# Windowed attention feeding a gated feed-forward layer: weight loads, two casts, one copy and one batch's preparation moved in the order of work

## The chip, the cores and the metric

The kernel runs on one core of a Trainium2 chip. The metric is device time in microseconds (us); lower is better. Before the change, eight runs gave a median of 257.36 us (256.04 to 259.91). The profile shown below is of one execution that took 257.31 us.

## The reference

For 4 batches of 8 heads, 768 positions and head size 64, in fp32, attention is computed in which a query sees the first 4 positions and the 128 positions that end with itself; then a gated feed-forward layer runs over the 3072 tokens:

```
keep   = is_sink | in_window            # first 4 keys, or 0 <= q - k < 128
scores = where(keep, q @ k.T / 8, -1e9)
a      = softmax(scores);  x = (a @ v) with the heads side by side     # [3072, 512]
out    = (relu(x @ w_gate) * (x @ w_val)) @ w_out                      # d_ff = 1536
```

## The kernel before

**Units and stages.** Two heads make a *pair*; a batch has four pairs, so there are 16 units U0 to U15, four for each batch. Scores are formed only where the mask keeps them: keys are taken in seven overlapping tiles of 128. A unit passes these stages:

- its keys and queries are loaded in fp32 (`load_rows`, L159, through SyncE's DMA queue, called SP) and cast to bf16 by GpSimd (POOL) into `kn`, `qn` (`cast_rows`, L164);
- they are transposed. For batches 0 and 1 TensorE does it (`T_half`, `T`, L248), and ScalarE or VectorE copies the result from PSUM to SBUF (L258 the keys, L259 the queries). For batches 2 and 3 the casts are written to DRAM (`to_dram`, L169, "td") and come back by a transposing DMA (`turn`, L174), both on SP;
- `odd_tiles` (L183) has GpSimd copy some key columns once more, with the 4 sink keys in front;
- `Sg` (L279) forms scores for a third of the unit, ScalarE takes the exponential (L298) and VectorE multiplies by the mask (L300); these are S00, S01, S02 for the first pair of a batch, S10 to S12 for the second, and so on;
- `W` (L310) multiplies by the values `vn`; VectorE normalises (L330, L331). The values come in seven tiles j, each loaded by SP into one buffer `vf` (`load_v`, "lv") and cast by GpSimd (L134, "v");
- `X` (L334) transposes the result on TensorE and ScalarE copies it to `xT` (L345); for batches 2 and 3 it goes through DRAM instead (`x_to_dram` "xd", `x_turn` "xturn").

**The feed-forward part** is cut into 96 `chunk`s (L351), called slots: 24 for each batch, each with 4 products with the gate weights and 4 with the value weights (L362), a ReLU on ScalarE (L373) and a multiplication on VectorE (L375). Batch 0 is slots 0 to 23, batch 1 24 to 47, batch 2 48 to 71. Its second matrix product (`ffn2`, L400) is spread over later slots, three products a slot. The attention of batch b+1 is interleaved with the chunks of batch b: `plan` says after which slot which step stands, `prep` says before which slot a load, cast or copy is issued.

**What sets the order.** The order is written out by hand, and each engine, and each DMA queue, takes its own instructions in this order. A wait therefore holds everything behind it on that engine or queue. Three places matter here:

- GpSimd issues the weight loads itself (L190, L194), between its casts and copies.
- `pair()` (L239) hands out two PSUM tiles by turns. `T` takes one for its queries, and each `Sg` takes the next: after T of the third pair (T2) come S02 and then S10, and S10 gets the tile that T2's queries were in.
- In slots 0 and 8 the last pair's `X` stands in the middle of the chunk (`mid`): two gate and two value products come before it, the others after it. The fourth product of each kind reads what that `X` writes.

For units 8 and 9 the loads wait for a one-element write by VectorE (`gate`, L136), which stands in VectorE's order at the slot of the load.

In `prep`, a unit's four times are rows (load), castrows, td and turn. `rows` of unit 12, the first of batch 3, is at slot 30 throughout. Within a slot, units stand in rising order.

Of the kernel before, what the change touches and what calls it, by code (L numbers as in the profile page):

```python
# [21 lines left out]
def kernel(  # L22
# [12 lines left out]
    nc = tc.nc  # L35
# [5 lines left out]
    KO = d_model // 128  # L41
# [16 lines left out]
    qT = [x[:, 0:S] for x in KQ]  # L58
# [6 lines left out]
    wg = const.tile([128, KO, d_ff], BF16, name="wg")  # L65
    wv = const.tile([128, KO, d_ff], BF16, name="wv")
    wo = const.tile([128, FM, d_model], BF16, name="wo")
# [40 lines left out]
    half = lambda bufs, c: bufs[c // 2 % len(bufs)][:, c % 2 * HALF:c % 2 * HALF + HALF]  # L108
# [74 lines left out]
    def odd_tiles(u, copy):  # L183
        e = kE[u.i % NT]
        copy(odd(e)[:, :, 4:128], e[:, 120:876].rearrange("d (i c) -> d i c", c=252)[:, :, 0:124])  # L185
        sinks(u, copy)
# [52 lines left out]
    def pair():  # L239
        rot[0] += 1  # L240
        return PP[rot[0] % 2]
# [6 lines left out]
    def T(u):  # L248
        t = u.i % NT
        tk, tq = G[3][:], pair()[:, 0, :]  # L250
        for x, ps in ((kn[u.i % 2], tk), (qn[u.i % 2], tq)):
            for n in range(NR):
                c = slice(128 * n, 128 * n + 128)
                nc.tensor.transpose(ps.bitcast(BF16)[:, c], x[:, c], ident[:])
        vk, vq = (ps.bitcast(BF16)[:, 0:S].rearrange("d (n p) -> d p n", p=128) for ps in (tk, tq))
        e = kE[t]
        to = lambda ap: ap.rearrange("d (p n) -> d p n", n=NR)
        nc.scalar.copy(to(e[:, 0:S]), vk)  # L258
        (nc.scalar.copy if u.p < 2 else nc.vector.tensor_copy)(to(qT[t]), vq)  # L259
        odd_tiles(u, nc.gpsimd.tensor_copy)  # L260

    def T_half(c, banks=None, keys=nc.scalar.copy, queries=nc.vector.tensor_copy):
# [71 lines left out]
    def X(u, part=None, bank=None, copy=nc.scalar.copy):  # L334

        if bank is None:
            bank = G[3][:] if u.b == 0 or u.p < 2 else pair()[:, 0, :]
        ps = bank.bitcast(BF16)
        tiles, q0, q1 = PART[part]
        c = 0  # L340
        for t in tiles:
            nc.tensor.transpose(ps[:, c:c + 128], xn[u.i % 2][:, t, :], ident[:])  # L342
            c += 128 - t % 2 * 4
        c = 0 if part == 1 else 8
        copy(xT[u.b % 2][:, u.p, q0:q1], ps[:, c:c + q1 - q0])  # L345
        for x in range(2) if part is None else (part,):
            ready[u.b, u.p, x] = True
# [3 lines left out]
    def chunk(b, g, m, mid=None):  # L351

        x, h = xT[b % 2], hT[b % 2]
        cut = CUT if b else CUT0
        c = slice(0, cut) if g == 0 else slice(cut, S)
        n = c.stop - c.start
        gp, vp = G[gvn[0] % 3], G[(gvn[0] + 1) % 3]
        gvn[0] += 2

        def products(w, ps, kos):  # L360
            for ko in kos:
                nc.tensor.matmul(out=ps[:, 0:n], lhsT=w[:, ko, m * 128:(m + 1) * 128], rhs=x[:, ko, c],  # L362
                                 start=ko == 0, stop=ko == KO - 1)

        k0 = 2 if mid else 0
        if mid:
            products(wg, gp, range(k0))
            products(wv, vp, range(k0))
            mid()
        assert all((b, p, g) in ready for p in range(NP)), (b, g)  # L370
        products(wg, gp, range(k0, KO))
        gs = gspool.tile([128, S - CUT0], F32, name="gs")
        nc.scalar.activation(gs[:, 0:n], gp[:, 0:n], Act.Relu, bias=0.0, scale=1.0)  # L373
        products(wv, vp, range(k0, KO))
        nc.vector.tensor_tensor(h[:, m, c], gs[:, 0:n], vp[:, 0:n], op=Alu.mult)  # L375
# [31 lines left out]
    with tc.manual_schedule():  # L407
# [81 lines left out]
                for y in w.split():  # L489
                    put(s, y, b)  # L490
        prep = [[] for _ in slots]
        prep[1] += [("half", 6), ("half", 7), ("w", 6, 8), ("setup3",), ("v", 0, 3), ("v", 0, 4), ("v", 0, 5), ("v", 0, 6)]
        prep[4] += [("load", 4), ("load", 5), ("load", 6)]
        prep[8] += [("kq", 4), ("load", 7), ("lv", 1)]
        prep[9] += [("kq", 5), ("w", 8, 12)]
        prep[10] += [("kq", 6)]
        prep[11] += [("kq", 7)]
        prep[14] += [("v", 1, 0), ("v", 1, 1), ("v", 1, 2), ("v", 1, 3), ("wo",), ("v", 1, 4), ("v", 1, 5), ("v", 1, 6)]
        for i, ts in ((8, (18, 21, 22, 25)), (9, (19, 22, 23, 27)), (10, (21, 24, 25, 29)), (11, (23, 25, 27, 31)),
                      (12, (30, 33, 35, 38)), (13, (32, 35, 37, 40)), (14, (34, 37, 39, 43)), (15, (36, 39, 41, 45))):  # L500
            for t, what in zip(ts, ("rows", "castrows", "td", "turn")):
                prep[t].append((what, i))
            assert at["S", i - NP, 2] < ts[3] < at["S", i, 0] - 1, i
            prep[at["S", i, 0] - 1].append(("sinks", i))
            prep[at["W", i, 0] + 1].append(("xd", i))
            prep[at["W", i, 0] + 3].append(("xturn", i))

        for b, s0, s1 in ((2, 24, 28), (3, 44, 47)):
            for j in range(7):
                prep[s0 + j].append(("lv", b, j))  # L510
                prep[s1 + j].append(("v", b, j))

        f2 = deque()
        mid = {0: lambda: X(U[3], 0, g0), 8: lambda: X(U[3], 1)}
        for s, (b, g, m) in enumerate(slots):
            for x in prep[s]:
# [32 lines left out]
                else:  # L549
                    cast_v(*x[1:])  # L550
            chunk(b, g, m, mid.pop(s, None))
            if s == 23:
                f2 += [lambda t=t, mm=mm: ffn2(0, t, mm) for t in range(6) for mm in range(FM)]
            for what, i, x in plan[s]:
                if what == "F":
                    for _ in range(i):
                        f2.popleft()()
                elif what == "X":
                    X(U[i], x if i < NP else None)
                elif what == "T":  # L560
                    T(U[i])
                elif what == "H":
                    T_half(NP + i, queries=nc.scalar.copy if i == 0 else nc.vector.tensor_copy)
                elif what == "S":
                    Sg(U[i], x)
                else:
                    W(U[i], x if i < NP else None)
# [43 lines left out]
```

## Time and profile before

| what | value |
|---|---|
| the profiled execution's own time | 257.31 us |
| its span, first to last instruction | 255.3 us |
| TensorE (PE) busy | 241.3 us, 95% |
| weight loads on TensorE (PEld) | 140.8 us, 55% |
| VectorE (DVE) / ScalarE (ACT) / GpSimd (POOL) busy | 116.9 / 120.4 / 70.1 us |
| DMA | 40.07 MB, mean 157 GB/s |
| granted TensorE clock, mean | 0.984 |

By stretches of the span, in us:

| stretch | what runs | PE busy | ACT busy | POOL busy | DMA share |
|---|---|---|---|---|---|
| 0 to 20 | batch 0, first scores | 14.53 | 10.24 | 13.67 | 1.03 |
| 20 to 42.5 | slots 0 to 8 | 21.48 | 15.45 | 11.19 | 1.15 |
| 42.5 to 66 | slots 9 to 19, batch 1's T and S | 21.96 | 20.23 | 17.21 | 0.77 |
| 66 to 77 | slots 20 to 23, batch 1's W and X | 11.00 | 4.16 | 3.31 | 1.09 |
| 77 to 102 | slots 24 to 35, batch 2's S | 25.00 | 13.34 | 8.11 | 1.09 |
| 102 to 136 | batch 2's W, batch 3's loads | 31.81 | 13.39 | 9.79 | 0.99 |
| 136 to 160 | batch 3's S | 23.58 | 13.94 | 6.82 | 0.50 |

PE's busy time is modelled at the ends of matmuls, and stretches of matmuls overlap in it. A DMA share near or above 1 says that the 16 DMA engines had packets under way all the time. In rows of a timeline the first number is the start in us from the span's start, the second how long the row lasted; brackets hold the idle time of the engine before it and what ended that.

### The profile page before, as it was taken

Reading aid. Unit: us, or ns where it says so; the run is one execution under the profiler, and the core shown is the slowest. Engines: PE = TensorE matmul, PEld = TensorE weight load, DVE = VectorE, ACT = ScalarE, POOL = GpSimd, SP = SyncE. Lnnn points to the kernel's source line nnn. Section 1 sums busy time; section 2 is a strip of 40 time slices with the busy share of each in tenths; the row PEclk is TensorE's granted clock in tenths of the full one; section 3 lists DMA queues with packets and bytes.
Section 4 is the critical chain, followed back from the end, with each engine's and each line's share of the span. In section 5 each row is a group of like instructions: output and inputs, shape, how many; then the busy total and the mean of one; then the engine's idle time right before and its main releaser. Section 6 shows DMA issues by size and latency. Waiting matters only on the chain.

```text
span 255.3 us, 5322 instructions
## 1 busy us (share of the span) xinstructions
PE 241.3 (95%) x2084; PEld 140.8 (55%) x2084; DVE 116.9 (46%) x225; ACT 120.4 (47%) x219; POOL 70.1 (27%) x125
## 2 busy tenths in 40 slices
PE   7869999899999999699999999999999999999994
PEld 2444676555775555466655556666555555555443
DVE  5561794488872354467424455654223222322000
ACT  3744976789453385255234673622333233333111
POOL 7744941949054322733001720000000000000000
PEclk9995999999999999999999999999999999999999
DMA  6999999964999999999999902334210011110232
GB/s 214 223 202 259 200 371 236 183 111 67 194 384 283 251 216 253 256 315 255 165 237 218 203 3 64 88 89 121 74 44 17 24 41 44 44 41 0 85 122 83
DMA packets 75681, 40.07 MB, mean 157 GB/s; under 512 B 53512, under 2 KB 72712, under 8 KB 75656
## 3 DMA queue, kind: packets, MB, share of 16 engines
q1 hardware_dynamic: 67560, 34.10, 51.4%
q0 software_dynamic: 6864, 4.72, 12.7%
q10 hardware_dynamic: 1232, 0.92, 1.1%
q8 instruction: 16, 0.26, 0.4%
q14 instruction: 9, 0.07, 0.1%
HBM read 28.48 MB, written 11.25 MB: 156 GB/s over the span
## 4 chain that ended last, share of the span: by engine, by line
PE 71%; DMA 11%; SPq 7%; issue 5%; POOL 2%; ACT 1%; DVE 1%; ACTq 0%; POOLq 0%; DVEq 0%
PE g L362 39%; PE g L400 19%; DMA qf<-in_q_dram 7%; SPq L131 5%; PE pp L325 4%; PE pp L290 3%; PE pp L400 3%; DMA kf<-in_k_dram 3%; DMA vf<-in_v_dram 1%; SPq L113 1%; POOL qn L166 1%; SPq L175 1%; ACT ee L298 1%; SPq L161 1%; PE pp L394 1%
## 5 line engine op out<-in xcount | busy, mean ns | idle before, releaser
L375 DVE TENSOR_TENSOR hT<-gs,g 128x384 bf16<-128x384 f32 (+2 forms) x96 | 53.0, 552 | 92.4 <-PE g L362 87.4
L373 ACT ACTIVATE gs<-g 128x384 f32<-128x384 f32 (+2 forms) x96 | 47.5, 495 | 74.7 <-PE g L362 73.5
L362 PE MATMUL g<-xT,wg 128*128 128x384 bf16 (+2 forms) x384 | 79.9, 329 | 1.5 <-DMA wg<-in_moe_w_gate_dram 0.9
L362 PE MATMUL g<-xT,wv 128*128 128x384 bf16 (+2 forms) x384 | 79.7, 330 | 1.4 <-DMA wv<-in_moe_w_val_dram 1.3
L400 PE MATMUL g<-wo,hT 128*128 128x512 bf16 x240 | 64.0, 379 | 0.2 <-ACT ot L404 0.2
L362 PEld LDWEIGHTS <-wg 128*128 128x128 bf16 x384 | 36.3, 99 | 31.4 <-DMA wg<-in_moe_w_gate_dram 1.0
L362 PEld LDWEIGHTS <-wv 128*128 128x128 bf16 x384 | 37.7, 99 | 28.3 <-issue 2.3
L298 ACT ACTIVATE ee<-pp 128x838 bf16<-128x838 f32 (+4 forms) x50 | 43.1, 904 | 12.6 <-PE pp L290 12.4
L300 DVE TENSOR_TENSOR ee<-ee,msk 128x838 bf16<-128x838 bf16 (+3 forms) x44 | 32.4, 743 | 13.5 <-ACT ee L298 13.2
L400 PEld LDWEIGHTS <-hT 128*128 128x128 bf16 x276 | 25.5, 98 | 23.6 <-issue 0.4
L134 POOL CAST vn<-vf 128x512 bf16<-128x512 f32 x27 | 18.5, 704 | 24.5 <-DMA vf<-in_v_dram 24.3
L325 PEld LDWEIGHTS <-ee 128*128 128x128 bf16 x512 | 17.9, 97 | 4.9 <-issue 2.9
L404 ACT COPY ot<-g 128x512 f32<-128x512 f32 x20 | 11.7, 587 | 17.5 <-PE g L400 17.5
L325 PE MATMUL pp<-vn,ee 128*128 128x65 bf16 x488 | 17.8, 193 | 2.2 <-POOL vn L134 2.2
L290 PEld LDWEIGHTS <-KQ 64*128 64x128 bf16 x328 | 11.0, 94 | 11.5 <-issue 8.8
L166 POOL CAST kn<-kf 128x768 bf16<-128x768 f32 x12 | 10.4, 869 | 25.0 <-DMA kqd<-kn 9.4
L331 DVE TENSOR_TENSOR xn<-pp,rn 128x896 bf16<-128x896 f32 (+2 forms) x18 | 17.0, 943 | 0.6
L290 PE MATMUL pp<-KQ 64*128 64x3 bf16 (+5 forms) x316 | 16.2, 222 | 0.8 <-DVE KQ L259 0.6
L166 POOL CAST qn<-qf 128x768 bf16<-128x768 f32 x12 | 11.1, 924 | 2.3 <-DMA qf<-in_q_dram 1.9
L185 POOL COPY KQ<-KQ 128x372 bf16<-128x372 bf16 x12 | 6.4, 534 | 16.7 <-ACT KQ L258 9.8
L345 ACT COPY xT<-g 128x372 bf16<-128x372 bf16 (+2 forms) x10 | 5.4, 544 | 8.9 <-PE g L342 8.9
L400 PE MATMUL pp<-wo,hT 128*128 128x512 bf16 x36 | 8.1, 379 | 0.0
(80 smaller groups left out, 106.8 us busy)
## 6 DMA issues: line engine op xcount, KB each, us to landing
out_dram<-ot SPq DMA_DIRECT2D x23, 256.0 KB
kf<-in_k_dram SPq DMA_DIRECT2D x12, 384.0 KB
qf<-in_q_dram SPq DMA_DIRECT2D x12, 384.0 KB
vf<-in_v_dram SPq DMA_DIRECT2D x12, 256.0 KB
vf<-in_v_dram SPq DMA_DIRECT2D x12, 224.0 KB
kf<-in_k_dram SPq DMA_DIRECT2D x8, 192.0 KB
wo<-in_moe_w_out_dram POOLq DMA_DIRECT2D x3, 512.0 KB, 7.6
kqd<-qn SPq DMA_DIRECT2D x8, 192.0 KB
```

The lines of the kernel that those rows point to most:

```text
L131: nc.sync.dma_start(out=vf[a0:a1, j, :, :], in_=v[b, :, s0:s0 + a1 - a0, :].rearrange("h s d -> s h d"))
L134: copy(vn[b % 2][0:rows, j, :, 0:64], vf[0:rows, j, :, :])
L166: nc.gpsimd.tensor_copy(dst[u.i % 2][:].rearrange("p (n h d) -> p h n d", n=NR, h=2), src[u.i % NQ][:].rearrange("p (h n d) -> p h n d", n ...
L290: nc.tensor.matmul(out=at[h][:, c0:c1], lhsT=kE[t][64 * h:64 * h + 64, x0:x0 + 128], rhs=qT[t][64 * h:64 * h + 64, q0:q0 + c1 - c0], start ...
L298: nc.scalar.activation(x, ps[:, :, b0:n], Act.Exp, bias=0.0, scale=scale)
L300: nc.vector.tensor_tensor(x, x, msk[:, g, b0:n].unsqueeze(1).to_broadcast([128, 2, n - b0]), op=Alu.mult)
L325: nc.tensor.matmul(out=at[h][:, c:c + 65], lhsT=ee[u.i % NE][:, g, h, c0:c0 + 128], rhs=vn[u.b % 2][:, j, 2 * u.p + h, 0:65], start=c == 0 ...
L331: nc.vector.tensor_tensor(x.rearrange("p t (h d) -> p h t d", h=2), o[:, :, :, 0:64], r.unsqueeze(3).to_broadcast([128, 2, n, 64]), op=Alu ...
L362: nc.tensor.matmul(out=ps[:, 0:n], lhsT=w[:, ko, m * 128:(m + 1) * 128], rhs=x[:, ko, c], start=ko == 0, stop=ko == KO - 1)
L373: nc.scalar.activation(gs[:, 0:n], gp[:, 0:n], Act.Relu, bias=0.0, scale=1.0)
L375: nc.vector.tensor_tensor(h[:, m, c], gs[:, 0:n], vp[:, 0:n], op=Alu.mult)
L400: nc.tensor.matmul(out=op, lhsT=hT[b % 2][:, m, t * 128:(t + 1) * 128], rhs=wo[:, m, :], start=m == 0, stop=m == FM - 1)
```

## The change

Six places are edited.

1. `chunk` with a `mid`: after the `X`, the third gate and the third value product now both come before the fourth gate product (slots 0 and 8).
2. Slot 1: the load of weight blocks 6 and 7 stands in GpSimd's order between the cast of half 6 and that of half 7, in place of after both.
3. Slot 8: the cast of unit 5 ("batch 1's second cast") and the load of weight blocks 8 to 11 move from slot 9 to slot 8. On GpSimd they now stand ahead of the odd-tile copies of unit 4.
4. The queries of batch 1's third pair (unit 6) are copied from PSUM by ScalarE in place of VectorE (L259).
5. The load of the output weights moves from slot 14, where it stood among the value casts, to slot 13; on GpSimd it stands ahead of the odd-tile copies of unit 7.
6. Batch 2: rows, castrows, td and turn of units 8 to 11 are each a slot sooner, and so are the loads of batch 2's values (their casts stay). Unit 12's rows stay at slot 30: SP now has unit 11's turn ahead of them, and the first output tile and the last values' load also change places with their neighbours there.

```diff
-        (nc.scalar.copy if u.p < 2 else nc.vector.tensor_copy)(to(qT[t]), vq)
+        (nc.scalar.copy if u.p < 3 else nc.vector.tensor_copy)(to(qT[t]), vq)
...
         assert all((b, p, g) in ready for p in range(NP)), (b, g)
+        if mid:
+            products(wg, gp, range(k0, KO - 1))
+            products(wv, vp, range(k0, KO - 1))
+            k0 = KO - 1
         products(wg, gp, range(k0, KO))
...
-        prep[1] += [("half", 6), ("half", 7), ("w", 6, 8), ("setup3",), ("v", 0, 3), ("v", 0, 4), ("v", 0, 5), ("v", 0, 6)]
+        prep[1] += [("half", 6), ("w", 6, 8), ("half", 7), ("setup3",), ("v", 0, 3), ("v", 0, 4), ("v", 0, 5), ("v", 0, 6)]
         prep[4] += [("load", 4), ("load", 5), ("load", 6)]
-        prep[8] += [("kq", 4), ("load", 7), ("lv", 1)]
-        prep[9] += [("kq", 5), ("w", 8, 12)]
+        prep[8] += [("kq", 4), ("load", 7), ("lv", 1), ("kq", 5), ("w", 8, 12)]
         prep[10] += [("kq", 6)]
         prep[11] += [("kq", 7)]
-        prep[14] += [("v", 1, 0), ("v", 1, 1), ("v", 1, 2), ("v", 1, 3), ("wo",), ("v", 1, 4), ("v", 1, 5), ("v", 1, 6)]
-        for i, ts in ((8, (18, 21, 22, 25)), (9, (19, 22, 23, 27)), (10, (21, 24, 25, 29)), (11, (23, 25, 27, 31)),
+        prep[13] += [("wo",)]
+        prep[14] += [("v", 1, 0), ("v", 1, 1), ("v", 1, 2), ("v", 1, 3), ("v", 1, 4), ("v", 1, 5), ("v", 1, 6)]
+        for i, ts in ((8, (17, 20, 21, 24)), (9, (18, 21, 22, 26)), (10, (20, 23, 24, 28)), (11, (22, 24, 26, 30)),
                       (12, (30, 33, 35, 38)), (13, (32, 35, 37, 40)), (14, (34, 37, 39, 43)), (15, (36, 39, 41, 45))):
...
-        for b, s0, s1 in ((2, 24, 28), (3, 44, 47)):
+        for b, s0, s1 in ((2, 23, 28), (3, 44, 47)):
```

## The prediction, made before the change was run

> **What bounds the kernel now.** I read the page, the waits of PE, PE's timeline at each wait, and then the timelines of the engine or queue that ended it.
>
> ```profile
> PE 241.3 (95%) x2084; PEld 140.8 (55%) x2084; DVE 116.9 (46%) x225; ACT 120.4 (47%) x219; POOL 70.1 (27%) x125
> ...
> PEclk9995999999999999999999999999999999999999
> DMA  6999999964999999999999902334210011110232
> ```
>
> PE is the bound: 255.3 - 241.3 = 14.0 us idle is all that moving work can win. Slices are 6.38 us; DMA has room only in slices 8 and 9 (51 to 64 us) and after 140. PE's waits by releaser:
>
> ```profile
> PE pp L325 <- POOL vn L134: 2.2, 2, 1.3
> ...
> PE g L254 <- POOL kn L166: 0.7, 1, 0.7
> PE g L362 <- ACT xT L345: 0.7, 2, 0.4
> PE pp L290 <- DVE KQ L259: 0.6, 1, 0.6
> ...
> PE pp L254 <- POOL qn L166: 0.3, 1, 0.3
> ```
>
> These add up to 4.5 us, and each is touched. The other idle time lies before 20 us, in gaps too short to be listed, and at the end. The biggest wait, batch 2's first W (102.2 to 105.1 us), is ended by GpSimd:
>
> ```profile
> 101.58 0.83 POOL L166 CAST kn<-kf 128x768 bf16<-128x768 f32 x1 [4.96 <-DMA kf<-in_k_dram]
> 102.56 0.83 POOL L166 CAST qn<-qf 128x768 bf16<-128x768 f32 x1
> 103.33 0.61 POOL L134 CAST vn<-vf 128x512 bf16<-128x512 f32 x1
> ...
> 104.46 0.61 POOL L134 CAST vn<-vf 128x512 bf16<-128x512 f32 x1
> ```
>
> The last two value tiles stand behind unit 12's cast, which GpSimd awaits for 4.96 us: the load, not the cast, is late. SP shows why:
>
> ```profile
> 92.13 3.02 SPq L175 DMA_TRANSPOSE KQ<-kqd  x1
> 95.20 1.22 SPq L131 DMA_DIRECT2D vf<-in_v_dram  x3
> 96.46 0.56 SPq L161 DMA_DIRECT2D kf<-in_k_dram  x1
> 97.06 0.46 SPq L161 DMA_DIRECT2D qf<-in_q_dram  x1
> 97.57 0.40 SPq L131 DMA_DIRECT2D vf<-in_v_dram  x1
> 98.07 0.36 SPq L405 DMA_DIRECT2D out_dram<-ot  x1
> 98.53 3.69 SPq L175 DMA_TRANSPOSE KQ<-kqd  x1
> 102.27 0.57 SPq L161 DMA_DIRECT2D kf<-in_k_dram  x1
> ```
>
> Those rows belong to slot 30, which PE began at 89.8 us; SP is 6.6 us behind and has no gap. So W's end is set by SP, not by PE: what PE gains earlier counts there only as far as unit 12's load also comes sooner.
>
> **Part by part, up to 66 us.**
>
> *Split products (1).* PE waits 0.25 us (20.74 to 20.99, slot 0) and 0.41 (41.59 to 42.00, slot 8) for `xT`. One value product now stands ahead of the wait: about 0.31 us at slot 0, where the clock was 0.5 (22.51 to 23.75 for four), 0.17 at slot 8 (43.17 to 43.84 for four). It saves the smaller of wait and product: 0.25 + 0.17 = 0.42. The gate's ReLU starts as before, no product is added, and the multiplication behind waits for one value product instead of two; I see no reason for a loss.
>
> *Weights 6 and 7 sooner (2).* Two issues (0.74 and 0.75 us, at 25.95) move past half 7's two casts, to about 23.2. Half 7's casts were waiting for their loads (0.90 and 0.84 us idle before them), so they end as before, and PE transposes half 7 at 30.12, 4 us after. PE shows no wait for these weights at slot 6. I take nothing. [...] Bounds -0.3 (a wait that other executions may have there) to +0.3.
>
> *Unit 5's cast ahead (3).* T of unit 5 waits 0.68 + 0.26 = 0.94 us for casts at 44.47 and 45.24, because GpSimd held them for 6.63 us behind unit 4's odd tiles, which need ScalarE's copy at 43.03. Unit 4's queries were asked at 28.97 and cast at 36.08; unit 5's, asked at 30.23, should be there by 37.4, so both casts are done before 40, and the 0.94 us go. Two weight issues (1.5 us) come along and end near 40.5, before the odd tiles can start at 43.7: hidden by the same 6.63 us. Next late is T of unit 6: GpSimd does unit 5's odd tiles (0.65), then unit 6's casts (1.54), from ScalarE's copy at about 45.6: done at 47.9. PE gets there at 48.3. The cushion is 0.4 us; two casts beside VectorE's masks took 1.33 and 1.27 instead of 0.83, which would use it up: bounds 0 to +0.5, I take 0.
>
> *Queries by ScalarE (4).* S10 waits 0.56 us for VectorE's copy (51.85, 0.94 us), which reads the PSUM tile that S10 is to write. On ScalarE such a copy is 0.81 (43.73) and stands right behind the keys' copy, in front of slot 12's ReLU. By the sum it ends at 50.5, when PE reaches S10: the wait goes. [...] The price is that ScalarE, 20.23 us busy of 23.5 here, gets 0.81 more while PE needs less: 21.0 of 21.6. Behind the copy are slot 12's ReLU and all exponentials to slot 17. Those ran in pairs at about 0.9 each with 2 us of gaps, and gaps of 0.2 to 0.5 before each pair are what they now use. Bounds 0 to +0.8 (all of it lost); I take 0.
>
> *Output weights sooner (5).* Three issues (2.22 us) move past four value casts and unit 7's odd tiles, to about 51, before ScalarE's keys for those tiles (about 53.8). They fill the free slices 8 and 9. Free in itself; its worth is in 6: unit 8's keys, asked at 65.69, were cast only at 72.32, while loads in the clear (77.18 to a cast at 80.92) take 3.7.
>
> Sum: 0.42 + 0.94 + 0.56 = 1.9 us sooner at batch 1's first W, with an upper cost of 1.3.
>
> **Batch 2 a slot sooner (6).** Unit 8's gate leaves its place behind the masks of slot 17 (65.58) for one ahead of them, where a mask ends at 63.85; less 1.9, that is 62.0. With 3.7 us the cast starts at 65.7, against 72.32: 6.6 sooner. Unit 9's gate takes the old place, 63.7; its cast comes at 67.5 against 74.42. From unit 8's td (74.22) to the end of unit 11's turn (102.22) SP has no gap over 1.6 us, so I move that row of work by 6.6. But unit 11's turn is now ahead of unit 12's rows, which with the second output are 1.6 us: the turn ends at 102.22 - 6.6 - 1.6 = 94.0, and unit 12's rows go out at 94.1, only 2.4 sooner. Behind a turn, unit 13's rows took 3.7 us from issue to cast (102.27 to 106.01); unit 12's took 5.1. So its cast starts at 97.8 to 99.2, and 3.5 us later (101.58 to 105.07) the last value tile is there: 101.3 to 102.7. PE begins W at 102.19 - 1.9 = 100.3 and needs that tile at about 101.0. Of 2.2 us of waits 0.3 to 1.7 stay. PE left the last wait at 105.13; it now leaves between 101.3 and 102.7, 2.4 to 3.8 sooner. I take 3.3, since the DMA engines have less ahead of unit 12. Nothing between there and the end takes it back: unit 8's xd waits for W itself (SP idle to 107.26), so the chain xd to xT moves along, and its DMAs meet fewer loads.
>
> Sum against the profiled execution: 257.31 - 3.3 = 254.0 us; that execution is within 0.1 of the median, 257.36.
>
> **The rivals.**
>
> *A, the likeliest:* as above, 252.7 to 255.0 (at best all 4.1 us, plus 0.5 of small waits behind).
>
> *B, SP gains less.* Rows 64 to 102 are at 9 tenths of DMA or more; if that throughput, not the start, sets SP's pace, the chain moves by 4 to 5 us in place of 6.6, and PE by 1.3 to 2.3: 255.0 to 256.0. For it: turns took 1.71 to 3.69 us, so they were held up. Against: the output weights leave that stretch.
>
> *C, no change.* `xT` of batch 2's last pair is turned at 132.41 for 1.14 us and slot 48 uses it at 134.74: PE is just behind it. If SP does not come sooner from 107 to 133, all is given back there: 257.3. Against: SP's own wait for W.
>
> *D, slower.* Unit 12's rows wait behind unit 11's turn. If the chain in front gains nothing, they go out at 96.46 + 3.69 + 0.5 = 100.7, 4.2 us later; with the shorter landing, W ends 2.9 later: 260.2. It loses once the chain gains under 2.9 us. For it: those 4.2 us are certain. Against: 6.6 is more.
>
> **How the numbers follow.** A 0.62, B 0.19, C 0.09, D 0.10. Half a per cent, 1.29 us, is about what a measurement of this kernel can tell from no change. A and B are faster by more (0.81), C within (0.09), D slower (0.10). Range: from 252.6 to 256.4, the end of B with some of C; D and the rest of C are left out.
>
> **What would show it.** Right: no PE wait on L254 by L166 or on L290 by L259; waits for `xT` of about 0 and 0.25; the first W's wait for L134 at 0.3 to 1.7; SP issues unit 12's rows near 94 and unit 8's cast is near 66. Wrong: ScalarE ends more PE waits between 48 and 66; unit 12's cast is not before 100; a new wait for `xT` at slot 48.

## The result, and the profile after

The changed kernel takes 253.04 us (median of 18 executions, 251.29 to 255.13) against 257.3 us for the kernel before beside it (53 executions): 0.9863 times as long, 95% interval 0.9838 to 0.9888, so 1.4% faster. The ratio leaves out the executions that are more than 1.5% above the fastest of their kernel; the medians are of all executions. In a second measurement (experiment e5) it was 0.9863 again, 0.9798 to 0.9928. The profiled execution took 253.48 us, its span is 251.5 us; before it was 257.31 and 255.3.

The profile of the changed kernel, in the same rows as the first ones shown of before (slices are 6.29 us now):

```profile
PE 240.4 (96%) x2084; PEld 140.9 (56%) x2084; DVE 116.3 (46%) x224; ACT 120.6 (48%) x220; POOL 70.9 (28%) x125
...
PEclk9997999999999999999999999999999999999999
DMA  6999999999979999899999511333211011110232
```

PE is as busy as before and idle for 11.1 us in place of 14.0. The hole in the DMA row at slices 8 and 9 (51 to 64 us) is closed; there is one small hole in slice 11, and more room from slice 22 on. PE's waits by releaser (us in total, times, longest):

```profile
PE pp L325 <- POOL vn L134: 2.0, 4, 0.9
...
PE g L325 <- POOL vn L134: 0.7, 2, 0.4
PE g L362 <- DMA wg<-in_moe_w_gate_dram: 0.6, 1, 0.6
PE g L362 <- ACT xT L345: 0.5, 2, 0.2
```

The waits of L254 for casts and of L290 for VectorE's copy are gone. The wait of W for values is nearly as large in sum, 2.0 after 2.2 us, but it lies elsewhere. PE's timeline shows where (start, duration; in brackets the idle time before and what ended it):

```profile
34.23 0.22 PE L325 MATMUL pp<-vn,ee 128*128 128x65 bf16 x2 [0.20 <-POOL vn L134]
35.15 1.12 PE L325 MATMUL pp<-vn,ee 128*128 128x65 bf16 x32 [0.70 <-POOL vn L134]
...
64.04 0.70 PE L325 MATMUL pp<-vn,ee 128*128 128x65 bf16 x18 [0.24 <-POOL vn L134]
...
101.55 0.70 PE L325 MATMUL pp<-vn,ee 128*128 128x65 bf16 x18 [0.91 <-POOL vn L134]
```

Batch 2's first W waits 0.91 us, not 2.19. Two are new: 0.90 us in batch 0's W, 0.24 us in batch 1's. GpSimd's and SP's rows behind the wait at 101.55:

```profile
64.50 0.83 POOL L166 CAST kn<-kf 128x768 bf16<-128x768 f32 x1 [0.52 <-DMA kf<-in_k_dram]
...
98.02 0.83 POOL L166 CAST kn<-kf 128x768 bf16<-128x768 f32 x1 [7.00 <-DMA kf<-in_k_dram]
...
100.88 0.61 POOL L134 CAST vn<-vf 128x512 bf16<-128x512 f32 x1
```

```profile
67.74 0.37 SPq L171 DMA_DIRECT2D kqd<-qn  x1
...
87.68 2.07 SPq L175 DMA_TRANSPOSE KQ<-kqd  x1
89.80 1.77 SPq L131 DMA_DIRECT2D vf<-in_v_dram  x4
91.66 1.55 SPq L175 DMA_TRANSPOSE KQ<-kqd  x1
93.25 0.59 SPq L161 DMA_DIRECT2D kf<-in_k_dram  x1
93.89 0.47 SPq L161 DMA_DIRECT2D qf<-in_q_dram  x1
```

Unit 8's cast starts at 64.50 in place of 72.32. Unit 12's rows now stand behind unit 11's turn and go out at 93.25 in place of 96.46; their cast is at 98.02 in place of 101.58, and the last value tile is there at 101.49. The rows at 67.74, 87.68 and 91.66 (unit 8's td, and the turns of units 10 and 11) come back below.

PE's lead over the kernel before, by the start of the same instruction in both traces:

| at | before | after | lead |
|---|---|---|---|
| slot 0's fourth gate product | 20.99 | 19.81 | 1.18 |
| slot 6 | 34.18 | 32.41 | 1.77 |
| slot 7 | 36.66 | 36.10 | 0.56 |
| T of unit 4 | 42.50 | 41.65 | 0.85 |
| slot 10 | 46.47 | 44.33 | 2.14 |
| slot 13, batch 1's first W | 53.18, 66.06 | 50.33, 63.21 | 2.85 |
| batch 2's first W | 102.19 | 99.73 | 2.46 |
| after it, slot 48 | 105.76, 134.74 | 102.18, 131.16 | 3.58 |
| end of the span | 255.3 | 251.5 | 3.8 |

The first 1.18 us are not the change's alone: the first weights came sooner in this execution (PE waited 0.96 and 0.6 us for them, before 1.31 and 0.87), and PE's clock was granted at half from 19.8 to 23.2 us, before from 18.5 to 25.3.

### The profile page after: what moved, and what is told of

It reads as the page before. It is cut to its first block, busy times and chain, and to the rows that moved or that the text cites. A ratio compares the mean times of both kernels' runs of the same rounds, so it can differ in the third digit from the quotient of the medians.

```text
span 251.5 us, 5321 instructions
## 1 busy us (share of the span) xinstructions
PE 240.4 (96%) x2084; PEld 140.9 (56%) x2084; DVE 116.3 (46%) x224; ACT 120.6 (48%) x220; POOL 70.9 (28%) x125
## 4 chain that ended last, share of the span: by engine, by line
PE 70%; DMA 16%; SPq 7%; POOL 2%; issue 1%; ACTq 0%; ACT 0%; DVE 0%; POOLq 0%; DVEq 0%
PE g L362 37%; PE g L404 20%; DMA vf<-in_v_dram 10%; SPq L131 7%; PE pp L325 5%; DMA kf<-in_k_dram 4%; PE pp L404 3%; PE pp L290 2%; DMA qf<-in_q_dram 2%; POOL vn L134 2%; SPq L161 1%; PE pp L398 1%; PE g L398 1%; PE g L342 0%; ACTq L113 0%
## 5 line engine op out<-in xcount | busy, mean ns | idle before, releaser
L134 POOL CAST vn<-vf 128x512 bf16<-128x512 f32 x27 | 19.3, 725 | 33.1 <-DMA vf<-in_v_dram 33.1
L290 PEld LDWEIGHTS <-KQ 64*128 64x128 bf16 x328 | 10.8, 94 | 10.3 <-issue 8.0
L290 PE MATMUL pp<-KQ 64*128 64x3 bf16 (+5 forms) x316 | 15.9, 221 | 0.0
```

Source lines behind the costliest of these rows:

```text
L134: copy(vn[b % 2][0:rows, j, :, 0:64], vf[0:rows, j, :, :])
L290: nc.tensor.matmul(out=at[h][:, c0:c1], lhsT=kE[t][64 * h:64 * h + 64, x0:x0 + 128], rhs=qT[t][64 * h:64 * h + 64, q0:q0 + c1 - c0], start ...
```

## The experiments

Each of e1 to e12 but e5 is the changed kernel with the named part undone or added, or the kernel before with one part alone. Ratios are to the kernel before measured beside them (e1 to e4: 258.22 us, e5 to e8: 256.46 us, e9 to e12: 257.64 us; since these medians differ, a ratio of e1 to e4 looks lower than its time alone would). My theory is the prediction's: SP's issue of unit 12's rows sets the end of batch 2's first W, and what moves those rows moves the time. This table compares it with all profiles. Absolute positions carry the luck of the first 25 us, so columns two and three count from batch 1's first W (start of W4) in the same profile: unit 8's cast, and SP's issue of unit 12's rows. The fourth is PE's wait in batch 2's first W.

| kernel | cast of unit 8 | rows of unit 12 | wait | ratio [95%] |
|---|---|---|---|---|
| before | 6.3 | 30.4 | 2.19 | 1 |
| whole change, first profile | 1.3 | 30.0 | 0.91 | 0.9863 [0.9838, 0.9888] |
| e5, whole change again | 1.2 | 29.7 | 0.92 | 0.9863 [0.9798, 0.9928] |
| e1, without edit 6 | 2.9 | 28.6 | 0.38 | 0.9766 [0.9719, 0.9813] |
| e2, edit 6 alone | 6.2 | 33.9 | 5.46 | 1.0127 [1.0083, 1.0172] |
| e3, without edit 2 | 1.0 | 29.4 | 0.91 | 0.9773 [0.9726, 0.9821] |
| e4, whole, unit 12's rows first | 1.3 | 26.9 | 0 | 0.9737 [0.9691, 0.9784] |
| e6, edit 5 alone | 2.7 | 28.8 | 0.75 | 0.9928 [0.9888, 0.9968] |
| e7, without edit 5 | 6.5 | 33.0 | 4.58 | 1.0101 [1.0049, 1.0152] |
| e8, without edit 4 | 0.9 | 29.2 | 0.49 | 0.9881 [0.9807, 0.9954] |
| e9, without edit 3 | 0.8 | 28.6 | 0.71 | 0.9879 [0.9819, 0.9939] |
| e10, without edit 1 | 1.6 | 29.3 | 0.92 | 0.9844 [0.9776, 0.9911] |
| e11, rows first, without edit 2 | 1.3 | 27.8 | 0 | 0.9787 [0.9739, 0.9836] |
| e12, as e4, again | 1.2 | 27.3 | 0 | 0.9797 [0.9737, 0.9857] |

Up to 27.8 us there is no wait; from 28.6 to 30.0 it is 0.4 to 0.9, at 30.4 2.2, at 33 and 34 4.6 and 5.5. So the wait goes with the third column, not with the second. e5 is the whole change measured once more, beside e6 to e8:

> The whole change once more, beside the next kernels. Theory, that leaving edit 6 out and moving unit 12's rows were real gains: its ratio to the kernel before is again 0.984 to 0.989 (about 253.0 to 254.5 us), and the first W of batch 2 waits 0.7 to 1.2 us. Rival, that the lower times of those two came from their chip: the ratio is 0.974 to 0.979, as theirs.

**e1 and e2: batch 2's place.** e1 puts edit 6 back, e2 makes it alone.

```diff
-(8, (17, 20, 21, 24)), (9, (18, 21, 22, 26)), (10, (20, 23, 24, 28)), (11, (22, 24, 26, 30)),
+(8, (18, 21, 22, 25)), (9, (19, 22, 23, 27)), (10, (21, 24, 25, 29)), (11, (23, 25, 27, 31)),
-for b, s0, s1 in ((2, 23, 28), ...
+for b, s0, s1 in ((2, 24, 28), ...
```

> Edits 1 to 5 without edit 6 (batch 2 keeps its old slots). My theory, that SyncE's queue and the place of unit 12's rows in it set the end of batch 2's first W: the output weights are still out of the way, VectorE reaches the old places of the gates about 2.9 us sooner, so unit 8's cast starts near 66.5 us (after the whole change 64.5, before it 72.3) and unit 12's rows, again ahead of unit 11's turn, go out near 91 us (93.3 after the whole change). No wait is left at batch 2's first W, and the time is about 252.3, no worse than the whole change. Rival: moving batch 2 a slot is what frees that W; without it the wait there grows to 2 to 4 us, as PE comes sooner, and the time is 255.0 to 257.0.

> Edit 6 alone on the kernel before. My theory: the loads of unit 8 are asked about 1.8 us sooner but still stand behind the output weights, so its cast comes at most 1.5 us sooner; unit 12's rows now wait behind unit 11's turn, go out 0 to 3 us later than at 96.5, and the first W's wait is 2.2 to 5 us: 257.3 to 259.5. Rival: being a slot sooner is enough by itself: the first W waits under 1 us and the time is 255.3 to 256.0.

e1: 251.94 us. SP's rows of e1, with unit 12's in front of unit 11's turn:

```profile
89.47 1.23 SPq L131 DMA_DIRECT2D vf<-in_v_dram  x3
90.74 0.56 SPq L161 DMA_DIRECT2D kf<-in_k_dram  x1
91.34 0.46 SPq L161 DMA_DIRECT2D qf<-in_q_dram  x1
91.85 0.40 SPq L131 DMA_DIRECT2D vf<-in_v_dram  x1
92.81 3.62 SPq L175 DMA_TRANSPOSE KQ<-kqd  x1
```

Without edit 6 unit 12's rows go out 2.5 us *sooner* than with it (1.4 counted from W4), and the wait is shorter. Unit 8's cast is hardly later (65.00 after 64.50): the earlier gate brings half a microsecond to a microsecond and a half, the changed order costs more. e2: 261.12 us. The page's clock row, and PE at batch 2's first W:

```profile
PEclk9999979999999999589999999999999999999999
```

```profile
102.09 0.53 PE L325 MATMUL pp<-vn,ee 128*128 128x65 bf16 x12
107.21 0.27 PE L325 MATMUL pp<-vn,ee 128*128 128x65 bf16 x2 [4.59 <-POOL vn L134]
108.34 1.15 PE L325 MATMUL pp<-vn,ee 128*128 128x65 bf16 x18 [0.87 <-POOL vn L134]
```

Alone, edit 6 is a loss: the wait grows by 3.3 us, and SP issues the rows at 99.84, 3.4 later than before. That is rival D's mechanism. The time is higher than the 257.3 to 259.5 expected: the wait is longer than the 2.2 to 5 us given, and the clock is halved behind it (last section).

**e4 and e12: unit 12's rows a slot sooner**, so that they stand ahead of unit 11's turn again, with the whole change around them.

```diff
-(12, (30, 33, 35, 38))
+(12, (29, 33, 35, 38))
```

> The whole change with unit 12's rows at slot 29, ahead of unit 11's turn. Theory: the rows go out near 91.2 us in place of 93.3, the cast starts near 95.5 to 96.5, the first W's wait of 0.9 us goes and the time is 252.0 to 252.4. Rival: the wait passes to the values or to unit 11's odd tiles, which come later by what the rows take (1.1 us): 252.8 to 253.3.

> The whole change with unit 12's rows at slot 29, measured once more. Theory: the first W of batch 2 waits under 0.3 us and the ratio to the kernel before is 0.970 to 0.982, below the whole change's 0.986. Rival: the first time was its chip's luck: 0.984 to 0.989.

251.25 and 251.29 us, below the 252.0 to 252.4 expected of e4, with the rows at 90.80 and 89.78. GpSimd in e4:

```profile
94.57 0.83 POOL L166 CAST kn<-kf 128x768 bf16<-128x768 f32 x1 [3.91 <-DMA kf<-in_k_dram]
```

The wait at batch 2's first W is 0 in both. One line gives 1.7 us more than the whole change by medians, 1.4 by means (251.6 of the 12 executions of e4 and e12, 253.0 of the 24 of the whole change and e5). The interval of e12 alone overlaps that of the whole change. With e11, which has the line too, these are the fastest versions measured, ahead of both kernels.

**e6 and e7: the output weights.** e6 moves them alone, e7 leaves them where they were in the changed kernel:

```diff
-prep[13] += [("wo",)]
-prep[14] += [("v", 1, 0), ("v", 1, 1), ("v", 1, 2), ("v", 1, 3), ("v", 1, 4), ...
+prep[14] += [("v", 1, 0), ("v", 1, 1), ("v", 1, 2), ("v", 1, 3), ("wo",), ("v", 1, 4), ...
```

> Edit 5 alone (the output weights a slot sooner) on the kernel before. Theory: unit 8's loads meet free DMA engines, its cast starts near 69.5 us instead of 72.3, SyncE's row of work moves by 2.5 to 3 us with unit 12's rows still ahead of unit 11's turn (93.5 to 94 us), and most of the 2.2 us of wait at batch 2's first W go: 255.2 to 256.0 against 257.3 before. Rival: the DMA engines set SyncE's pace anyway, and nothing moves: 257.0 to 257.6.

> The whole change without edit 5 (the output weights again among the value casts of slot 14). Theory: unit 8's loads stand behind them, its cast starts near 69.5 to 70 us in place of 64.5, unit 12's rows, behind unit 11's turn, go out near 98.5, the first W's wait grows from 0.9 to about 5 us, and the time is 256.8 to 258.5: the gain of the whole change is gone. Rival: edit 5 is a small help; 253.0 to 254.0.

255.17 and 259.08 us. Unit 8's cast in e6, then in e7:

```profile
66.00 0.83 POOL L166 CAST kn<-kf 128x768 bf16<-128x768 f32 x1 [6.61 <-DMA kf<-in_k_dram]
```

```profile
70.73 0.83 POOL L166 CAST kn<-kf 128x768 bf16<-128x768 f32 x1 [8.20 <-PE g L342]
```

In e6 the load asked at 62.90 was cast 3.1 us later; in e7 the one asked at 62.12 needed 8.6. The bracket in e7 names PE, but the load is the likelier cause, for the output weights are under way at that time. The DMA view of e7 from 58 to 75 us (busy share in 40 slices of 0.43 us; below, an issue with its size and the median us to landing), and the same row of e6:

```profile
DMA  0005399999999999999999999999999999999998
...
wo<-in_moe_w_out_dram POOLq DMA_DIRECT2D x3, 512.0 KB, 7.7
```

```profile
DMA  9999985210100069999977999999999984239977
```

e7 starts the three loads of 512 KB at 57.75, and unit 8's, asked at 62.12, meets them; in e6 the engines have run empty by then. So nearly all of the sooner cast comes from edit 5. Without it all of the gain is gone, and the kernel is slower than before, because edit 6's order is still there. (The median of e7 is above the 256.8 to 258.5 expected; its profiled execution took 260.47 us, and these rows lie ahead of its halved clock, last section.)

**e3 and e11: weights 6 and 7.** e3 puts them behind half 7's cast again, e11 does so in e4's kernel.

```diff
-prep[1] += [("half", 6), ("w", 6, 8), ("half", 7), ...
+prep[1] += [("half", 6), ("half", 7), ("w", 6, 8), ...
```

> The whole change without edit 2 (weight blocks 6 and 7 again after both halves' casts). Theory: those weights took the DMA engines from batch 0's last values; without edit 2 the waits of W for the values cast at L134 near 34 us (0.2 and 0.7 us) go, the casts end near 33, and the time is 0.5 to 1.2 us lower, 251.9 to 252.6. Rival: the late values are that execution's own, and without edit 2 the value weights of block 6 come just as late: a wait for weights of 0.3 to 1.0 us near 32.5 us, 253.0 to 253.6.

> Unit 12's rows at slot 29 and weight blocks 6 and 7 back after both halves' casts: the whole change with one addition and without edit 2. Theory: edit 2 only changes which of two transfers PE awaits near slot 6 (values or value weights, about 1 us either way), so this equals the kernel with unit 12's rows first, within 0.4 us. Rival: edit 2 costs 0.5 us or more, and this is the fastest of all, by 0.5 us.

In e3 batch 0's W has no wait for its values. PE now waits just ahead of it, in slot 6's value products (e3, then e11):

```profile
34.93 0.81 PE L362 MATMUL g<-xT,wv 128*128 128x372 bf16 x4 [1.08 <-ACT gs L377]
```

```profile
32.85 0.80 PE L362 MATMUL g<-xT,wv 128*128 128x372 bf16 x4 [1.33 <-DMA wv<-in_moe_w_val_dram]
```

The bracket in e3 names ScalarE, e11's names the weights at the same place. The product follows the issue of its weights by 8.0 us in e3 and 8.3 in e11, so I read both as a wait for weights. e11 waits 0.39 + 1.33 us for weights; e12, which has edit 2, 0.75 us for weights and 0.75 + 0.34 for values: 1.72 and 1.84. In e5, the whole change again, it is 0.94 for weights and 0.25 + 0.34 for values. e11 and e12, side by side, took 251.38 and 251.29 us. So edit 2 moves part of the wait from the weights to the values; that it shortens the sum is not shown. e3's low ratio is not explained by a wait that it lacks, and e11 did not repeat it; part of it is that the kernel before took 258.22 us beside e3, 0.9 more than beside the whole change.

**e8, e9, e10: edits 4, 3 and 1 undone, one at a time.**

```diff
-(nc.scalar.copy if u.p < 3 ...                               # e8
+(nc.scalar.copy if u.p < 2 ...
-prep[8] += [..., ("lv", 1), ("kq", 5), ("w", 8, 12)]         # e9
+prep[8] += [..., ("lv", 1)]
+prep[9] += [("kq", 5), ("w", 8, 12)]
-        if mid:                                              # e10
-            products(wg, gp, range(k0, KO - 1))
-            products(wv, vp, range(k0, KO - 1))
-            k0 = KO - 1
```

> The whole change without edit 4 (the third pair's queries on VectorE again). Theory: S10 waits 0.5 to 0.8 us for VectorE's copy once more, all behind it comes that much later, gates included, and the time is 0.4 to 0.8 us higher than the whole change beside it. Rival: ScalarE, fuller with the copy, takes as much elsewhere: no difference, within 0.2 us.

> The whole change without edit 3 (unit 5's cast and weight blocks 8 to 11 again in slot 9). Theory: T of unit 5 waits about 1 us for its casts once more, the gates come 1 us later, PE and SyncE's row of work shift together, and the time is 0.8 to 1.4 us above the whole change's 253.0. Rival: PE's loss is hidden by the 0.9 us that it waits at batch 2's first W anyway, as SyncE sets its end: within 0.3 us of 253.0.

> The whole change without edit 1 (slots 0 and 8 as before). Theory: the two waits for xT are 0.25 to 0.4 us each again instead of 0.24 each, one product more stands behind each, and the time is 0.3 to 0.5 us higher, which these rounds can hardly tell from nothing. Rival: none of it reaches the end, as DMA landings set PE's pace between slots 0 and 8: 0.0.

253.30, 254.06 and 252.54 us. In each the wait that the edit took away is back: S10's in e8, T of unit 5 in e9, `xT` in slot 8 in e10 (0.41 us, against 0.24 in the whole change).

```profile
49.54 0.39 PE L290 MATMUL pp<-KQ 64*128 64x244 bf16 x6 [0.99 <-DVE KQ L259]
```

```profile
44.47 0.51 PE L254 MATMUL g<-ident,kn 128*128 128x128 bf16 x6 [0.69 <-POOL kn L166]
45.25 0.51 PE L254 MATMUL pp<-ident,qn 128*128 128x128 bf16 x6 [0.27 <-POOL qn L166]
```

In time none of the three can be told from the whole change; the intervals overlap. The waits say why at least in part: where PE comes later by 0.99 and 0.96 us, batch 2's first W waits less, 0.49 and 0.71 us in place of 0.92. Edits 3 and 4 pay in full only when unit 12's rows no longer set that time.

## Why the prediction was right

It gave 254.0 us, 0.81 for faster, and 3.3 us less for the profiled execution; that took 3.8 less, the median 4.3. Point by point:

**What sets the end of batch 2's first W** was right, with luck in one number: the value casts stand behind unit 12's cast, and that behind SP. "The turn ends at 94.0, and unit 12's rows go out at 94.1": 93.21 and 93.25. Cast "97.8 to 99.2": 98.02. Last tile "101.3 to 102.7": 101.49. "0.3 to 1.7 stay": 0.91. Lead after the wait 2.4 to 3.8: 3.58. From there nothing was given back: slot 48 has no wait for `xT`, so rival C fell.

**SP's row of work, and rival B.** That the turn ended near 94.0 is two errors that cancel. SP did not keep the 6.6 us. Unit 8's td did come 6.5 sooner, at 67.74; before it was here:

```profile
74.22 0.37 SPq L171 DMA_DIRECT2D kqd<-qn  x1
```

But unit 10's turn came only 4.5 sooner (92.13, 87.68), which is the 4 to 5 of rival B. Unit 11's turn so began at 91.66, 1.3 later than the sum has it (94.0 - 3.69 = 90.3). It still ended in time, since it held SP for 1.55 us in place of the 3.69 that the sum took from before. That was not luck of one execution: the turn takes 1.45 to 1.66 us in all 8 profiles in which unit 12's rows stand behind it, and 2.93 to 3.69 in the 6 in which they stand ahead. Why is not shown. With so short a turn the 4.2 us that D calls certain were not certain either. Whether it was the DMA engines that held SP up, as B has it, is open. (B's 1.3 to 2.3 us for PE are worked from the best case of A, not from the 3.3 taken.)

**The lead at batch 1's first W** is 2.85 us for the 1.9 predicted, but 1.77 of it stood at slot 6, mostly from the first weights and the clock: luck of this execution. From there on edits 1, 3 and 4 gave 2.3 for the 1.67 predicted, and edit 2's wait took 1.2 back.

**Who earns it** was partly wrong. The step "6.6 sooner" of unit 8's cast came out (7.8), but I wrote it under edit 6 with its gates. By e6 and e1 it is edit 5: the output weights alone bring unit 8's cast from 6.3 to 2.7 us behind W4, edit 6 a further 1.6, while it puts unit 12's rows 2.7 to 3.0 us further behind that cast (28.7 in the whole change, 25.7 to 26.0 in e1 and e6). By the waits, edit 6 costs about half a microsecond: 0.91 against 0.38. By medians it costs 1.1 us, but e1's executions had a fuller clock (mean 0.999, the whole change 0.995); those at 0.997 or more took 251.9 us (5 of e1) and 252.1 (10 of the whole change and e5). So nothing shows edit 6 to pay inside the change, which is as fast without it; whether it costs 0.2 or 1.1 us there is open.

**Rival D** had the right place and price: 260.2 if the chain in front gains nothing; e2, where it gains 0.2 us, took 261.1 and e7 259.1. It did not come true since unit 8's cast gained far more than its 2.9 us.

**Edit 2, "I take nothing",** failed. Batch 0's last two value tiles were cast from 33.30 to 35.10, W took the others from 33.68, and PE waited 0.90 us there; the bound of +0.3, which no run shows, was too small (and the upper cost of 1.3 leaves it out: the bounds add up to 1.6). The weights were asked 2.6 us sooner (24.08 for 26.68), with a DMA share of 1.18 from 20 to 42.5 us, and GpSimd waited 2.85 us for those two tiles; in e11, without the edit, W begins at 33.49 and waits for none. That the weights held the values back is my reading of this. But e3 and e11 show that without the edit PE waits 1.08 and 1.72 us for the weights: I had missed that too, since the trace of before, in which PE was slower up to there, has no wait at slot 6. The two errors about cancel.

**Edits 1, 3, 4.** Edit 1: at slot 0 the wait of 0.24 us stays although a product now stands ahead of it (at half clock before, at full clock now), at slot 8 it falls from 0.41 to 0.24: 0.17 of the 0.42 predicted. Edit 3: the lead grows by 1.29 us from T of unit 4 to slot 10, 0.94 was predicted. Rows of PE overlap: after, the keys' transposes of unit 5 follow at 43.66 a row that ends at 43.82, so a listed wait is short of the loss by about 0.16 us, and there were two. Edit 4: 0.71 from slot 10 to slot 13, 0.56 was predicted, one wait. ScalarE was busy 20.26 us of 23.5 from 42.5 to 66 and ends no wait of PE there: the cost of 0 to 0.8 was rightly taken as 0. The VectorE copy of e8 still held S10 for 0.99 us.

**"Free in itself"** for edit 5, and "hidden" for edit 3's weights, were not quite so. Both loads now go out ahead of batch 1's last values: GpSimd waits 5.01 us for these at 62.81, and PE 0.24 us at 64.04. GpSimd waits there in 8 of the 9 profiles with both edits and in none of the 5 without one of them; PE has a listed wait in 3 of the 9, of 0.24 to 0.45 us.

**What the profile does not show in one execution: the clock.** Every execution's mean granted clock is listed. In the 51 executions of the kernel before beside the experiments it is 0.991, in 24 of the changed kernel 0.995. Where PE is the bound, a mean clock lower by 0.0042 (the unrounded difference) costs by estimate that share of 253 us, about 1.1. Among executions at 0.997 or more the means are 255.5 (12) and 252.1 us (10), 3.4 apart; from 0.990 to 0.997, 257.1 (21) and 253.5 (12), 3.6 apart. So the path gave about what was predicted, and most of the remaining 0.9 us goes with a clock that is halved less often. Why it is, is open; only profiles tell where a halving lies, and the two profiles have theirs before 26 us.

## What to carry to other kernels

On a queue that issues in order, find the one transfer whose landing ends the wait, and judge a change by where it puts that transfer in the queue; moving a whole stage "a slot sooner" moved its own other DMAs ahead of the critical load. A bulk load moved into idle DMA time was worth more here than each moved cast or copy (without it e7 took 259.08 us, without edits 3 and 4 e9 and e8 took 254.06 and 253.30). Check a bundle with each part left out: this one held a part that alone costs 1.3% and brings nothing that can be seen inside the bundle, and one line more than the bundle was the better kernel. A sum that comes out can hide two errors: check its steps in the trace, not only its end.

## What the runs showed of the hardware

In e2 and e7 PE's time was lost twice at batch 2's first W, once in a wait and once under a halved clock. The granted clock is 0.5 from 105.0 to 111.8 us, in and behind waits of 4.59 and 3.67 us. By stretches, e7 (PE, PEld, DVE, ACT, POOL busy; PEclk; DMA share; GB/s):

```profile
104.00:105.00 1.00, 0.22 (x2) 0.12 (x2) 0.00 (x0) 0.00 (x0) 1.00 (x3) 1.00 1.04 289
105.00:108.40 3.40, 2.50 (x26) 1.69 (x27) 1.34 (x2) 0.99 (x1) 2.80 (x6) 0.50 0.96 357
108.40:111.80 3.40, 3.40 (x17) 1.48 (x17) 1.07 (x2) 0.51 (x2) 1.60 (x2) 0.50 0.62 169
111.80:113.00 1.20, 1.20 (x17) 0.65 (x12) 0.22 (x2) 1.10 (x2) 0.00 (x0) 0.98 0.98 248
```

Waits of 2.19 us (before, in two pieces) and 0.91 us (after) at the same place left the clock at 1.00. But one long wait is not needed: in the 3.4 us ahead of the halving at 19.8 (after) no listed wait was longer than 0.96 us. What goes before each of these four halvings is little PE work in the 3.4 us ahead of it: busy for 1.6 us (after, from 16.4), 1.8 (before, from 15.1), 1.0 (e2) and 0.2 (e7, both from 101.6). They lasted 3.4 us (after, 19.8 to 23.2) or 6.8 us (before, e2, e7). But little PE work is not enough: in before, PE is busy for only 1.21 us from 101.73 to 105.13, and the clock is 1.00 there and in the 3.4 us behind it. What decides whether a halving follows is not shown. Of the executions of e2 and e7, 21 of 24 had a mean clock below 0.990, of the kernel before 18 of 51, of the changed kernel 2 of 24.
